# Two interleaved layers of long convolutions on one core: the order of issue taken from two stored tables

## The chip, the cores and the metric

The kernel runs on one core of one Trainium2 chip. The metric is the device time of one execution in microseconds, the median over the runs shown. A core has a matrix engine (PE, TensorE), a vector engine (DVE, VectorE), a scalar engine (ACT, ScalarE), a general engine (POOL, GpSimd) and a queue engine (SP, SyncE) which here issues nearly all transfers. Each engine works through its own instructions strictly in the order in which they were issued to it; they meet at semaphores.

## The reference

The input x has 2048 positions and 512 channels. Four layers are added to it in turn, A, B, A, B, each fed with the layer norm of x:

```python
def _A_ref(q, k, v, shift_k, ssm_k, ssm_D):        # gate by q, filter given
    k_shift = causal convolution of k with 4 taps per channel
    kv = k_shift * v
    y = causal convolution of kv with ssm_k, 2048 taps per channel (FFT)
    return q * (y + kv * ssm_D)
def _B_ref(u, log_A_real, A_imag, C_real, C_imag, log_dt, D_skip):
    dt = exp(log_dt); A = -exp(log_A_real) + 1j * A_imag; C = (C_real + 1j * C_imag) * dt
    K[d, l] = 2 * Re sum_n C[d, n] * exp(A[d, n] * dt[d] * l)          # 128 modes, 2048 taps
    return causal convolution of u with K (FFT) + u * D_skip
x = A_q
x = x + _A_ref(_layernorm(x), A_k, A_v, A_shift_k, A_ssm_k, A_ssm_D)
x = x + _B_ref(_layernorm(x), B_...)
x = x + _A_ref(_layernorm(x), A_k, A_v, A_shift_k, A_ssm_k, A_ssm_D)
x = x + _B_ref(_layernorm(x), B_...)
```

The convolution inside A does not depend on x, so both A layers share it: it is done once, and each A layer then only scales x by rows and channels. B's filter K is the same in both B layers as well.

## The kernel before

All data is float32. A convolution over 4096 points is a two-stage transform on TensorE, with 32 by 32 transposes on VectorE between the stages. Channels go in four quarters of 128, a quarter in four groups of 32.

The names of tiles, which the profile shows, are the way to follow the work:

- *The filter of B* (`taps`: `load_rows`, `mags`, `angles`, `waves`, `products`, `contract`): 64 steps. SP loads mode rows (`rw`) from a DRAM array (`rows_d`) that the setup has written; TensorE makes magnitudes (`pm`) and angles (`pa`); ScalarE takes exponentials (`m`) and sines (`ab`, `tt`); POOL and VectorE multiply (`xy`, `e`); TensorE sums over modes (`pk`); VectorE scales (`ks`) and SP stores the taps (`kdram`).
- *The two filters' spectra* (`spectrum_quarter`): load (`kk`), transform (`pf`, transposes to `zk`, `pu`), copy (`pc`), store in DRAM (`spec`). Quarter by quarter, A's from the input, B's from `kdram`.
- *kv of A* (`gated`): load (`kvt`), four products on POOL (`prod`) that TensorE adds up (`kv`), store (`kv_d`).
- *A convolution* (`convolution`, once for A, twice for B), 32 steps of four frequencies: `pf`, `zu`, `pu` forward; multiplication by the loaded spectrum (`kab`; `vv`, `sw`); inverse by `pi`, a copy (`zu` or `ie`), transposes (`w`), `po`. For A, `finish_a` keeps the result (`ya`, stored in `ya_d`) and updates the loaded quarter of x (`xq`, from which POOL has subtracted the row mean); a quarter of x is stored as `x1_d`.
- *Between the layers*: row statistics (`st`, `mv`), the normalizer (`var`, `rs`, `nb`) and normalized rows (`u`). The second A layer is `gated_update`.

None of this is issued in the order in which it is written. Engines are stand-ins: `record` (line 151) notes each operation with what it reads and writes. `flush` (line 475) asks `best` for an order, and then issues all operations in it, chaining those of each engine so that the order holds. There are two flushes. The first covers everything up to the normalized and transformed first quarter of the first B layer (2211 operations, of which the first 63 are setup that was issued directly); the second covers both B layers and the second A update (824 operations).

`plan` (line 279) is a list scheduler: at each step it takes, over all engines, the operation that can start first by the cost model, and among those of one engine with the same start the one with the lowest rank. `best` (line 442) first plans with the rank of recording, then 24 times with ranks made from the latest starts (`latest`) and the starts of the last plan, and keeps the plan with the shortest modelled length. `plan` also picks the buffer of the shared PSUM tiles (tags `c1`, one bank, and `f1`, two double banks in the first flush). The cost model is in `cost` (line 192): per operation the time that it occupies its engine, its latency, and for transfers the time on a common server.

## Time and profile before

| | us |
|---|---|
| median of 3 runs (671.56 to 673.98) | 671.78 |
| the profiled execution, its own time | 677.28 |
| its span from first to last instruction | 675.5 |
| first operations of the second flush in the trace | 456 |

The page of the profile gives busy time by engine, the span in 40 slices, the groups of instructions by operation and tile, and the transfers. As one helper records every operation, nearly all have one line (L487), so groups are told apart by tile names. Tiles that share a buffer can show under one name: `pm` and some `pu` of the first half stand as `pf`, and `po` as `kv`. A float32 matmul shows as two instructions. The stretches that the prediction uses are: up to 60 us the setup and the first spectra; to 236 us the filter of B, the spectra and kv together; to 408 us A's convolution beside the rest of B's filter; to 460 us the passage to the first B layer; to 510 and 578 us the first B convolution and the second A update; to 663 us the second B convolution; then the last outputs.

### The profile page before, as it was taken

To read this page: it belongs to the slowest core of one execution; us is meant where nothing else is said; L and a number is where in the kernel's file an instruction comes from. 1 tells how busy PE (TensorE), PEld (TensorE's weight loads), DVE (VectorE), ACT (ScalarE), POOL (GpSimd) and SP (SyncE) were. 2 spreads that over 40 slices of the span, in tenths; PEclk is the share of its full clock that TensorE was granted. 3 is DMA by queue.
4 is the path that set the end of the run, shared out by engine and by line. 5 is a ranking of instruction groups with operands and counts; after the bars stand their busy time and mean duration, and the time that the engine had idled before them with its cause. 6 is when DMAs were issued, how large, how long until landed. Compare 5 with 4: busy or idle time off the path is not lost. (4 is left out here: it accounts for less than half of the span.)

```text
span 675.5 us, 20764 instructions
## 1 busy us (share of the span) xinstructions
PE 532.5 (79%) x8568; PEld 300.0 (44%) x8568; DVE 472.1 (70%) x900; ACT 409.1 (61%) x770; POOL 352.9 (52%) x344
## 2 busy tenths in 40 slices
PE   1468979988999998888797884546989932799994
PEld 0123444534444366454555641414656601467571
DVE  7514746664467686798797896544569999898884
ACT  3304877886767799886557772355744408937341
POOL 3445887898879774551633554003536410366461
PEclk9969989998999999897998886657999965989998
DMA  7887997797877376469677743795677421077875
GB/s 214 219 227 217 258 225 247 220 257 172 231 230 242 119 252 215 140 169 270 207 258 188 235 143 91 224 318 207 257 277 250 163 94 62 2 244 250 294 236 109
DMA packets 74499, 138.97 MB, mean 206 GB/s; under 512 B 8092, under 2 KB 37156, under 8 KB 72356
## 3 DMA queue, kind: packets, MB, share of 16 engines
q1 hardware_dynamic: 73540, 135.21, 66.0%
q0 software_dynamic: 864, 2.43, 1.3%
q8 instruction: 68, 1.11, 0.7%
q14 instruction: 27, 0.22, 0.1%
HBM read 97.75 MB, written 39.85 MB: 204 GB/s over the span
## 5 line engine op out<-in xcount | busy, mean ns | idle before, releaser
L487 POOL TENSOR_TENSOR xy<-tt,m 128x512 f32<-128x512 f32 x128 | 148.6, 1184 | 87.8 <-issue 37.9
L487 POOL TENSOR_TENSOR sw<-sw,kab 128x512 f32<-128x512 f32 x64 | 81.3, 1291 | 104.4 <-ACT sw L487 93.6
L487 POOL TENSOR_TENSOR prod<-kvt 128x512 f32<-128x512 f32 x64 | 80.1, 1272 | 12.3 <-PE pf L487 4.2
L487 DVE STREAM_TRANSPOSE zu<-pf 128x512 f32<-128x512 f32 x96 | 62.7, 691 | 19.4 <-PE pf L487 16.3
L487 PE MATMUL kv<-prod,minus 128*128 128x512 f32 x128 | 72.3, 660 | 2.9 <-DVE prod L487 2.9
L487 PE MATMUL pf<-u,w 64*128 64x512 f32 (+1 forms) x200 | 60.5, 692 | 16.0 <-ACT u L487 11.2
L487 PE MATMUL pf<-kk,w 64*128 64x512 f32 x128 | 43.7, 720 | 31.8 <-DMA kk<-ssmk_in 19.3
L487 ACT COPY pc<-pf 128x512 f32<-128x512 f32 x64 | 35.8, 591 | 52.5 <-PE pf L487 34.1
L487 ACT COPY ie<-pi 128x1024 f32<-128x1024 f32 x32 | 32.4, 1013 | 53.1 <-PE pi L487 53.1
L487 DVE STREAM_TRANSPOSE zk<-pf 128x512 f32<-128x512 f32 x64 | 42.0, 694 | 32.1 <-PE pf L487 30.5
L487 ACT ACTIVATE m<-pf 128x1024 f32<-128x1024 f32 x48 | 47.7, 1027 | 23.4 <-PE pf L487 22.9
L487 DVE TENSOR_TENSOR vv<-pu,kab 128x512 f32<-128x512 f32 x64 | 41.8, 678 | 27.9 <-ACT sw L487 22.9
L487 DVE TENSOR_TENSOR e<-pa,m 128x512 f32<-128x512 f32 x64 | 43.4, 680 | 21.4 <-ACT pa L487 14.4
L487 ACT ACTIVATE ab<-pa 128x512 f32<-128x512 f32 x64 | 38.3, 598 | 28.4 <-PE pa L487 28.2
L487 PE MATMUL pi<-vv,mm 64*64 64x128 f32 x1024 | 52.9, 275 | 1.6 <-DVE vv L487 0.8
L487 DVE TENSOR_SCALAR y<-pa 128x512 fp32r<-128x512 f32 x64 | 43.1, 681 | 12.0 <-PE pa L487 11.2
L487 PE MATMUL pi<-sw,mm 64*64 64x128 f32 x1024 | 51.5, 269 | 0.0
L487 PE MATMUL pk<-xy,e 128*32 128x64 f32 x2048 | 45.3, 235 | 4.3 <-POOL xy L487 3.0
L487 PEld LDWEIGHTS pk<-xy,e 128*32 128x32 f32 x2048 | 34.8, 118 | 28.6 <-issue 16.9
L487 PE MATMUL pu<-zu,w 64*64 64x128 f32 x1024 | 35.5, 275 | 12.3 <-DVE zu L487 7.4
L487 ACT ACTIVATE u<-x,nb,rs 128x128 f32<-128x128 f32 x101 | 40.5, 483 | 7.5 <-DMA x<-x_d 6.3
L487 ACT COPY sw<-pu 128x1024 f32<-128x1024 f32 x32 | 32.1, 1013 | 21.0 <-PE pu L487 18.9
(121 smaller groups left out, 1088.1 us busy)
## 6 DMA issues: line engine op xcount, KB each, us to landing
kab<-spec SPq DMA_DIRECT2D x94, 512.0 KB, 4.8
spec<-pc SPq DMA_DIRECT2D x64, 256.0 KB, 4.4
kvt<-kv_in SPq DMA_DIRECT2D x32, 312.0 KB, 6.2
kk<-ssmk_in SPq DMA_DIRECT2D x32, 128.0 KB, 8.7
xr<-x_in SPq DMA_DIRECT2D x8, 512.0 KB, 6.3
kv_d<-prod SPq DMA_DIRECT2D x16, 256.0 KB, 3.1
kdram<-ks SPq DMA_DIRECT2D x64, 64.0 KB, 4.4
kk<-kdram SPq DMA_DIRECT2D x32, 128.0 KB, 2.8
```

The lines of the kernel that those rows point to most:

```text
L487: ins = getattr(self.engines[op.engine], name)(*a, **k).ins
```

## The change

Two lists are put into the kernel. A list names the recorded operations of one flush by their numbers (the place at which `record` met them), in an order over all engines. `best` no longer searches: it hands `plan` the rank of each operation in the list. `plan` still takes the earliest possible start first, so the list decides among operations of one engine that could start at the same time. `latest` and `TURNS` go. In the cost model, the rate of a transfer now depends on its direction and on the length of its contiguous pieces, a transfer takes 0.6 us longer, and one case of ScalarE's cost is counted otherwise. In `prepare`, a recorded operation now comes, for the plan, after the operations of its engine that were issued before it; `flush` makes no edge of that, as it does so between different engines alone.

```diff
+ORDERS = [
+    [
...
+        131, 72, 76, 73, 108, 89, 107, 85, 121, 74, 86, 115, 75, 232, 116, 153, 144, 88, 134, 112, 87, 135, 278,
+        145, 138, 132, 154, 139, 146, 130, 91, 155, 77, 133, 140, 95, 147, 123, 92, 141, 78, 136, 277, 97, 358,
+        137, 142, 122, 143, 93, 109, 231, 357, 117, 111, 94, 110, 276, 150, 118, 148, 149, 162, 158, 96, 322,
...
+        1860, 1853, 1859, 1852, 2004, 2073, 1884, 2042, 2002, 1885, 1858, 1855, 2043, 1886, 1856, 1857, 1894,
+        1889, 1861, 1895, 1888, 1887, 2005, 2076, 1891, 1893, 1900, 1892, 2003, 1890, 2077, 1911, 1910, 1901,
+        1955, 1909, 2078, 1896, 2079, 2008, 1956, 2045, 2009, 1912, 2044, 2046, 2006, 1957, 2047, 1902, 1960,
+        2048, 2007, 1905, 1903, 1904, 1906, 2049, 1907, 1965, 1908, 1959, 2051, 1966, 1958, 1964, 1962, 1974,
...
+    ],
+    [
...
+        147, 119, 152, 151, 141, 157, 156, 153, 158, 154, 166, 148, 142, 149, 177, 159, 162, 155, 173, 175, 167,
...
+        739, 741, 748, 747, 719, 752, 750, 740, 751, 759, 753, 758, 755, 746, 757, 762, 760, 754, 761, 733, 763,
+        768, 769, 756, 766, 767, 734, 764, 776, 765, 735, 770, 736, 772, 777, 786, 742, 773, 785, 779, 775, 798,
...
+    ],
+]
...
             size = 4 * int(np.prod([c for _, c in aps[0].ap]))
             run = min(self.run(x) for x in aps)
-            return (450 if op.engine == "D" else 600), 1500 + size / 290, size / (290 if run >= 512 else 200)
+            if aps[0].space != DRAM:
+                rate = 340 if run == 1024 else 228 if run == 1248 else 268 if run > 2000 else 279
+            else:
+                rate = 211 if run < 512 else 322 if run < 1024 else 350
+            return (450 if op.engine == "D" else 600), 1500 + size / rate, size / rate
...
-            if any(hasattr(k.get(x), "tensor") for x in ("scale", "bias")):
-                o = n / 1.2 + (186 if name == "activation" and len(big) == 1 else 280)
+            given = sum(hasattr(k.get(x), "tensor") for x in ("scale", "bias"))
+            if given:
+                o = n / 1.2 + (186 if given == 1 else 280)
...
         self.costs = [self.cost(op) for op in ops]
+        issued = {}
+        for op in ops:
+            if op.engine in issued:
+                op.ordered.append(issued[op.engine])
+            if op.ins is not None:
+                issued[op.engine] = op
...
             if op.calls[0][0] == "dma_start":
                 server = max(server, t + o) + extra
-                end[n] = max(t + o + 1500, server + 1200)
+                end[n] = max(t + o + 2100, server + 1800)
...
-    def latest(self):
...
-    TURNS = 24
-
     def best(self):
-        order = self.plan()
-        best = self.length, order, self.place, self.starts, self.ends
-        for turn in range(self.TURNS):
...
-        self.length, order, self.place, self.starts, self.ends = best
-        return order
+        return self.plan(list(np.argsort(ORDERS.pop(0))))
```

What the numbers named later are, in the first list: 128 to 131 row loads of B's filter (`rw`), 132 to 143 its first magnitudes (`pm`, `m`), 144 and 153 its first angles (`pa`), 162 the first product (`xy`), 73 and 86 the first `pf` groups of A's filter spectrum, 2002 to 2005 the four transfers of the last quarter of x (`xq`), 2006 to 2009 the subtractions on it, 2047 a store of `ya`, 2183 to 2204 the `pf` of the first B quarter, 2190 the second of them. In the second list: 162 to 175 statistics (`st`) of the first B layer, 735 and 736 stores of outputs, 756 and 761 the last loads of the spectrum (`kab`). A place on an engine, as the prediction uses it, is the rank of an operation among the recorded operations of its engine, counted from 0, in the list or in the trace of before.

More of the change, by code (lines that the diff above doesn't have):

```diff
@@ L440 @@
-    TURNS = 24
-    def best(self):
-        order = self.plan()
-        best = self.length, order, self.place, self.starts, self.ends
-        for turn in range(self.TURNS):
-            late, early = self.latest(), self.starts
-            if turn % 3 == 2:
-                place = sorted(range(len(late)), key=lambda n: late[n])
-                rank = [0.0] * len(late)
-                for i, n in enumerate(place):
-                    rank[n] = i + n
-            else:
-                rank = [l + (e if turn % 3 else l) for l, e in zip(late, early)]
-            order = self.plan(rank)
-            if order is None:
-                break
-            if self.length < best[0]:
-                best = self.length, order, self.place, self.starts, self.ends
-        self.length, order, self.place, self.starts, self.ends = best
-        return order
+    def best(self):
+        return self.plan(list(np.argsort(ORDERS.pop(0))))
```

28 lines of the change are left out of this document (removed), and 148 rows, old and new, of the table ORDERS.

## The prediction

> **What bounds the kernel now.** I read the page's busy shares first, then the table by stretches of time, and then the timeline of single engines in the stretches that are not full.
>
> ```profile
> span 675.5 us, 20764 instructions
> PE 532.5 (79%) x8568; PEld 300.0 (44%) x8568; DVE 472.1 (70%) x900; ACT 409.1 (61%) x770; POOL 352.9 (52%) x344
> ...
> 0.00:34.00 34.00, 9.55 (x15) 3.13 (x16) 20.73 (x33) 11.35 (x17) 13.27 (x27) 1.00 0.79 217
> 34.00:60.00 26.00, 17.07 (x97) 7.13 (x96) 7.87 (x16) 3.55 (x6) 12.91 (x15) 0.80 0.73 208
> 60.00:236.00 176.00, 165.00 (x1968) 77.83 (x1966) 102.82 (x175) 133.87 (x271) 144.99 (x137) 0.96 0.79 223
> 236.00:408.00 172.00, 147.82 (x2960) 93.42 (x2960) 143.51 (x259) 130.89 (x261) 83.56 (x79) 0.91 0.69 207
> 408.00:460.00 52.00, 26.26 (x264) 13.32 (x264) 24.90 (x72) 20.77 (x47) 7.28 (x10) 0.65 0.69 213
> 460.00:510.00 50.00, 41.52 (x914) 28.75 (x916) 32.03 (x48) 27.67 (x44) 25.17 (x20) 0.93 0.64 234
> 510.00:578.00 68.00, 41.94 (x686) 23.86 (x682) 64.32 (x184) 31.98 (x53) 20.24 (x20) 0.80 0.40 140
> 578.00:663.00 85.00, 78.13 (x1658) 51.28 (x1658) 71.50 (x113) 47.88 (x74) 42.88 (x38) 0.98 0.65 210
> ```
>
> Columns of a stretch: its length, then busy time of PE, PEld, DVE, ACT and POOL, the granted TensorE clock, the DMA share, GB/s. No engine bounds the whole. TensorE is full from 60 to 236 us (165.0 of 176, 94%) and nearly so from 578 to 663 (92%). VectorE is full from 510 to 578 (64.3 of 68, 95%). Between 236 and 408 TensorE (86%) and VectorE (83%) share the load and neither is full: 24 and 28 us of waits on one another. Before 60 and from 408 to 460 every engine is under 70%: latencies in a row. An order can gain only where nothing is full, or by moving work out of a full stretch into a free one. It removes no instruction, so the busy sums stay.
>
> **The change, part by part.** All sums are against the profiled execution: 675.5 us of span, 677.28 us of its own time, 5.5 above the median of 671.78.
>
> *Planner edits.* The transfer rates, the two added fixed 0.6 us, ScalarE's cost and the removed `latest` are arithmetic at build time; no edge comes from the new `issued` chain either, since `flush` writes `op.ordered` edges only between different engines. Cost 0. They act only through the order and through which PSUM buffer a shared tile gets.
>
> *Start of the first table.* Recorded numbers tell what is moved. On SP the row loads 129, 128 and 131 of the generator stand at places 7, 8 and 10 of the planned transfers; in the trace they were at 32, 37 and 31. On TensorE the first `pa` and `pm` matmuls (153, 144, 134) stand at places 2 to 4, against 18 to 20, ahead of all but two `pf` groups of the filter spectrum. On POOL the first `xy` product (162) is at place 14, against 33.
>
> ```profile
> 21.90 4.70 SPq L179 DMA_DIRECT2D rows_d<-hl  x3
> 47.13 3.43 SPq L487 DMA_DIRECT2D rw<-rows_d  x4
> DMA to landing us min/median/max: 2.1/3.1/4.1
> kk<-ssmk_in SPq DMA_DIRECT2D x32, 128.0 KB, 8.7
> 14.78 2.07 PE L487 MATMUL pf<-kk,w 64*128 64x512 f32 x2 [14.78 <-DMA kk<-ssmk_in]
> 26.52 5.62 PE L487 MATMUL pf<-kk,w 64*128 64x512 f32 x10 [9.68 <-POOL kk L487]
> 39.96 2.17 PE L487 MATMUL pf<-kk,w 64*128 64x512 f32 x4 [4.53 <-DMA kk<-ssmk_in]
> 50.03 1.13 PE L487 MATMUL pf<-kk,w 64*128 64x512 f32 x4
> 58.10 0.73 PE L487 MATMUL pf<-tg,rw 64*128 64x512 f32 x4
> 72.31 4.62 POOL L487 TENSOR_TENSOR xy<-tt,m 128x512 f32<-128x512 f32 x4
> ```
>
> The rows are in DRAM soon after 26.6 us (21.90 + 4.70), plus a store's landing, which no row gives; I take 4 us, an estimate from the 2.1 to 4.1 us of their loads. The loads then land between 34 (3.1) and 39 us (8.7, the median of the crowded `kk` queue). The first generator matmul starts then, not at 58.1; the way from it to the first `xy`, 72.31 - 58.10 = 14.2 us, stays: first `xy` at 47 to 54 us, some 20 us earlier. That is not 20 us of span. TensorE had done 9.55 + 17.07 = 26.6 us by 60 and then ran at 94%. In the new order it waits for the rows with two groups done, so `pf` and `kv` work that filled 26 to 58 us stands behind: it loses 34 - 28 = 6 to 39 - 28 = 11 us of filling, and gains what the earlier generator gives it, at most the 26.0 - 17.07 = 8.9 us it idled from 34 to 60. At 236 us the same work precedes the first convolution step in both orders. So this part lies between -9 and +11 us; I take 0, in the middle, because 94% leaves little. Cover: what stands behind the row loads on SP is `kvt` and `kk`, whose users move behind too.
>
> The stretch from 34 to 60 us has a granted clock of 0.80, and the two rows of four `pf` matmuls are 2.17 us at 40 and 1.13 at 50. The Trainium skill ("TensorE: Matmul & The Clock Gate", What's actually happening) says that the clock falls to half after an idle window of about 3.4 us and rises after a busy one; the two rows agree. By that rule a thinner start stays cold for longer, which is the second rival below.
>
> *Middle, 236 to 408 us.* The table moves the convolution ahead of the last filters' spectra: its `zu`, `pi` and `w` steps of quarter 1 move 15 to 35 places forward on TensorE, VectorE and ScalarE, `pk` and `pu<-zk` back by as many; at quarter 3 only 3 to 10 places are left. What can be gained is the idle of the fuller engine, 172 - 147.8 = 24 us, of which the forward moves can reach about the half that is not handed back by the end: bounds 0 and -12. I take -4, nearer to 0, since the displacement shrinks to a third at the end of the stretch.
>
> *End of the first table.* This is a chain that the trace shows whole:
>
> ```profile
> 393.30 0.34 SPq L487 DMA_DIRECT2D x_d<-xq  x1
> 397.90 1.25 SPq L487 DMA_DIRECT2D xq<-x_in  x2
> 402.44 0.36 SPq L487 DMA_DIRECT2D ya_d<-ya  x1
> 402.86 0.53 SPq L487 DMA_DIRECT2D xq<-x_in  x1
> 404.61 0.54 SPq L487 DMA_DIRECT2D xq<-x_in  x1
> 407.27 1.19 POOL L487 TENSOR_TENSOR xy<-tt,m 128x512 f32<-128x512 f32 x1 [0.49 <-POOL xy L487]
> 408.40 4.05 POOL L487 TENSOR_TENSOR xq<-xq,off 128x512 f32<-128x512 f32 x4
> 412.48 0.69 DVE L487 SCALAR_TENSOR_TENSOR xq<-kv,xq 128x512 f32<-128x512 f32 x1 [3.43 <-POOL xq L487]
> 435.66 2.77 SPq L487 DMA_DIRECT2D x<-x_d  x2
> 424.70 2.15 PE L487 MATMUL pf<-kk,w 64*128 64x512 f32 x4 [0.97 <-DMA kk<-kdram]
> 445.38 2.08 PE L487 MATMUL pf<-u,w 64*128 64x512 f32 x4 [10.52 <-ACT u L487]
> ```
>
> The last quarter of x is loaded in four pieces. After two, SP stood at the store of `ya` (402.44), whose copy was late, and the fourth piece left at 404.61. The table has all four in a row (2004, 2002, 2005, 2003), ahead of that store (2047): the fourth goes at about 397.9 + 4 x 0.6 = 400.3. That is 4.3 us earlier, and the four subtractions, VectorE's update, the store of x1 and its reload hang on it. Bounds 0 (POOL or the bank is late instead) and -4.3; I take -4.3, as VectorE waited 3.43 for exactly this. What is late next is the `w`, `po`, `ya` round. Behind the reload the table puts the normalizer and the `u` rows ahead of the spectrum's last `pc` copies, but one `pf` (2190) behind them: 0 us, bounds -3 (the `pf` idle of 10.52 is mostly the reload, which stays) and +5 (the last `pf` waits for four pairs of `pu`).
>
> *Second table.* Everywhere under ten places, except in two spots.
>
> ```profile
> 493.00:510.00 17.00, 0.00 (x0) 1.00 0.59 214
> 510.00:527.00 17.00, 2.92 (x13) 1.00 0.90 309
> 646.19 1.75 SPq L487 DMA_DIRECT2D out_dram<-yo  x2
> 648.71 7.32 DMA kab<-spec
> 656.05 0.69 DVE L487 TENSOR_TENSOR vv<-pu,kab 128x512 f32<-128x512 f32 x1 [0.39 <-DMA kab<-spec]
> ```
>
> The first two rows are the `st` statistics alone (VectorE's busy time in a stretch): none before 510 us, 2.92 us in the full stretch that follows. The table puts nine of them (162, 173, 175, 172 and others) up to 30 places forward, among work that ran at 507 to 514. VectorE has 50 - 32.0 = 18 us free from 460 to 510, so what is moved there shortens the full stretch: bounds 0 and -2.9, I take -2. Late next is the rest of VectorE's own row of work to 578. At the end, the last `kab` load (761) was issued at 648.71 behind two output stores, landed after 7.32 us, and VectorE waited for it. The table has it in front of those two: up to 648.71 - 646.19 = 2.5 us, if its buffer is free by then; I take -1.5, between -2.5 and 0.
>
> **Sum.** 0 - 4 - 4.3 + 0 - 2 - 1.5 = -11.8 us: 665.5 for an execution like the profiled one, 660.0 for the median. The ends add to -9 - 12 - 4.3 - 3 - 2.9 - 2.5 = -33.7 and +11 + 5 = +16; they will not all fall on one side. The forecast's own range is 646 to 668 us.
>
> **Rivals.**
> *The generator is the clock of the first stretch.* If the convolution's start at 236 us waits for POOL's products rather than for TensorE, the 20 us by which `xy` starts earlier come through. For it: POOL is 145.0 of 176 us busy there and starts late. Against: 82% is less than TensorE's 94%, and POOL's last `kv` products keep nearly their places. Half of the 20 us more: about 650 us. Chance 0.15.
> *A cold, thin start.* TensorE waits for the rows to 39 us and the eight groups behind run at the clock of the row at 39.96. It then brings 11 us less to 60 us, all paid at 94%: 671.8 - 11.8 + 11 = 671 us. For it: the `kk` queue's 8.7 us. Against: the row loads' own 3.1. Chance 0.11. This is also what no change would look like.
> *The last filter spectrum ends the first half (slower).* On POOL the table puts the four subtractions (2008, 2009, 2006, 2007) ahead of ten `xy` products, nine of which ran before them. If the x pieces land no earlier than now, POOL stands until 408.4 with those ten behind: 412.4 + 10 x 1.19 = 424 instead of 413.5, and the chain `pk`, `ks`, store, load, `pf` (now 424.70) slips by some 10 us, past the `u` work, with `pf` 2190 behind it. It decides from the point where the convolution is less than about 8 us ahead at 393 us. The gain of 4.3 is lost, the middle's 4 with it (it is its condition), and 10 is added: 671.8 - 3.5 + 10 = 678 us. For it: POOL runs in order and has ten products there. Against: the middle moves the convolution forward. Chance 0.16.
>
> **Chances.** Forecast 0.58, larger gain 0.15, cold start 0.11, slower 0.16. The range of 8 in 10 runs from 645 (the larger gain, nearly whole) to 677 us. Within 0.5% (668.4 to 675.1), about what a measurement of this kernel tells from no change, lies the cold start; above it the slow rival and a little of the cold start; the rest is faster.
>
> **What will show it.** In the changed profile: the first `rw` load at 30 us and the first `xy` at 47 to 54; TensorE's busy time by 60 us near 26 (the start is 0), under 20 (cold) or over 30; the first `pi` matmul before 236 us or not; four `xq` loads without a store between them, and `xq` subtractions within 8 us of the first load; `st` busy before 510; the last `kab` load issued before 647. The prediction is wrong if the busy shares from 60 to 236 fall, or if POOL waits for `xq` with `xy` behind it.

## The result: 0.77% faster, where 1.75% was forecast

| | before | changed |
|---|---|---|
| median, us (20 runs each) | 675.19 | 669.14 |
| lowest to highest | 670.01 to 687.34 | 664.66 to 677.50 |
| ratio changed to before, 95% interval | | 0.9923 (0.9894 to 0.9951) |
| span of the profiled execution, us | 675.5 | 666.4 |

The changed kernel is faster by 5.2 us (0.0077 x 675.19; 3.3 to 7.2 us by the interval). The medians, here and below, are over all runs, while the ratios leave out slow runs, those more than 1.5% above the fastest of the same kernel, so a ratio is not the quotient of two medians. The forecast was 11.8 us. In the 20 runs the kernel before has a median of 675.19 and not the 671.78 of the three runs that the forecast started from, so the time of 669.14 lies in the range given, and yet the step to it is 44% of the forecast. The two profiled executions differ by 9.1 us, more than the medians do.

The page's first lines of the changed kernel, and then the table by stretches as for the kernel before (length; busy time of PE, PEld, DVE, ACT, POOL; granted TensorE clock; DMA share; GB/s):

```profile
span 666.4 us, 20761 instructions
PE 525.2 (79%) x8568; PEld 292.3 (44%) x8568; DVE 474.5 (71%) x900; ACT 409.3 (61%) x770; POOL 352.5 (53%) x344
```

```profile
0.00:34.00 34.00, 5.85 (x8) 1.67 (x8) 19.03 (x31) 11.36 (x17) 10.83 (x25) 1.00 0.59 164
34.00:60.00 26.00, 20.50 (x118) 8.15 (x122) 7.53 (x12) 14.26 (x25) 13.63 (x13) 1.00 0.92 201
60.00:236.00 176.00, 167.39 (x2221) 81.22 (x2213) 112.02 (x196) 131.71 (x268) 152.26 (x145) 1.00 0.88 250
236.00:408.00 172.00, 142.57 (x2680) 85.14 (x2676) 140.13 (x249) 120.83 (x241) 78.11 (x74) 0.89 0.66 193
408.00:460.00 52.00, 26.37 (x329) 13.23 (x329) 26.70 (x77) 27.66 (x62) 11.39 (x12) 0.74 0.71 222
460.00:510.00 50.00, 45.44 (x1008) 30.41 (x1012) 39.03 (x64) 25.11 (x35) 25.29 (x21) 1.00 0.78 271
510.00:578.00 68.00, 43.73 (x641) 24.86 (x636) 61.27 (x179) 38.24 (x74) 17.43 (x21) 0.82 0.29 102
```

The work is the same. What differs early is the granted clock: 1.00 from 34 to 236 us, where the kernel before has 0.80 and 0.96. What differs late is little: the stretch from 408 to 460 is as empty as before (26.37 us of TensorE against 26.26).

Rows picked from the timelines of the changed kernel's engines, at the places that the prediction named (start, length, engine, operation; in brackets the idle time before it and what ended it):

```profile
13.75 12.71 SPq L345 DMA_DIRECT2D rows_d<-hl  x4
34.16 0.81 SPq L615 DMA_DIRECT2D rw<-rows_d  x2
42.19 4.95 POOL L615 TENSOR_TENSOR prod<-kvt 128x512 f32<-128x512 f32 x4 [15.45 <-DMA kvt<-kv_in]
50.46 2.31 POOL L615 TENSOR_TENSOR xy<-tt,m 128x512 f32<-128x512 f32 x2 [3.13 <-ACT tt L615]
227.20 0.45 PE L615 MATMUL pf<-vv,mm 64*64 64x128 f32 x8 [0.43 <-DVE zk L615]
384.50 2.60 SPq L615 DMA_DIRECT2D xq<-x_in  x4
393.66 4.03 POOL L615 TENSOR_TENSOR xq<-xq,off 128x512 f32<-128x512 f32 x4
417.76 1.78 SPq L615 DMA_DIRECT2D kdram<-ks  x4
421.73 0.56 SPq L615 DMA_DIRECT2D x<-x_d  x1
422.53 2.78 SPq L615 DMA_DIRECT2D kk<-kdram  x2
429.81 0.34 POOL L615 TENSOR_TENSOR kk<-kk,dr 1x32 f32<-1x32 f32 x1 [16.13 <-DMA kk<-kdram]
443.98 0.58 ACT L615 COPY pc<-pf 128x512 f32<-128x512 f32 x1 [2.09 <-DMA spec<-pc]
445.83 2.08 PE L615 MATMUL pf<-u,w 64*128 64x512 f32 x4 [3.94 <-ACT pc L615]
449.49 1.99 PE L615 MATMUL pu<-zu,w 64*64 64x128 f32 x32 [1.58 <-DVE zu L615]
```

The rows of the kernel before that answer to these and that the prediction did not show:

```profile
236.33 0.45 PE L487 MATMUL pf<-vv,mm 64*64 64x128 f32 x8 [0.74 <-DVE vv L487]
418.17 1.76 SPq L487 DMA_DIRECT2D kdram<-ks  x4
421.46 1.16 SPq L487 DMA_DIRECT2D kk<-kdram  x2
424.06 0.24 POOL L487 TENSOR_TENSOR kk<-kk,dr 1x32 f32<-1x32 f32 x1 [10.30 <-DMA kk<-kdram]
455.95 1.11 PE L487 MATMUL pu<-zu,w 64*64 64x128 f32 x32 [1.51 <-DVE zu L487]
```

Read as a lead over the kernel before, the rows tell the case. The generator's first `xy` leads by 21.9 us (72.31 - 50.46), the first `pi` (shown as `pf<-vv,mm`) by 9.1, the reload of x by 13.9 (435.66 - 421.73), and the first product of the second half by 6.5 (455.95 - 449.49). So half of what convolution A had won was gone 28 us later. The last filter's chain never had that lead: its last taps are stored at 417.76 instead of 418.17. It then fell 5.8 us behind: its `kk` loads stand on SP behind the first reload of x (422.53), and POOL has them at 429.81 instead of 424.06. Everything after hangs on it: the pairs `pu<-zk`, their evictions `pc`, which wait for the store of `spec` (443.98), and the last `pf<-u` (2190), which the table puts behind those pairs and which waits 3.94 us for a PSUM buffer.

### The profile page after: what moved, and what is told of

Same layout as the page of the kernel before. It is cut to its first block, busy times and chain, and to the rows that moved or that the text cites. A ratio compares the mean times of both kernels' runs of the same rounds, so it can differ in the third digit from the quotient of the medians.

```text
span 666.4 us, 20761 instructions
## 1 busy us (share of the span) xinstructions
PE 525.2 (79%) x8568; PEld 292.3 (44%) x8568; DVE 474.5 (71%) x900; ACT 409.3 (61%) x770; POOL 352.5 (53%) x344
## 4 chain that ended last, share of the span: by engine, by line
PE 35%; DVE 17%; ACT 9%; DMA 8%; issue 4%; POOL 2%; SPq 1%; DVEq 0%; ACTq 0%; POOLq 0%
PE pf L615 11%; PE pi L615 6%; PE kv L615 6%; DMA kab<-spec 5%; PE po L615 4%; PE pu L615 3%; PE pa L615 3%; DVE zu L615 3%; DVE st L615 3%; PE pk L615 3%; DVE x L615 2%; DVE vv L615 2%; ACT tt L615 2%; ACT m L615 1%; DVE sw L615 1%
## 5 line engine op out<-in xcount | busy, mean ns | idle before, releaser
L615 PE MATMUL pf<-kk,w 64*128 64x512 f32 x128 | 45.8, 729 | 42.3 <-DMA kk<-kdram 14.8
L615 PE MATMUL pf<-u,w 64*128 64x512 f32 (+1 forms) x200 | 56.7, 651 | 13.3 <-ACT pc L615 3.9
L615 ACT ACTIVATE tt<-pa 128x256 f32<-128x256 f32 x128 | 46.6, 387 | 22.4 <-PE pa L615 22.1
L615 ACT COPY sw<-pu 128x1024 f32<-128x1024 f32 x32 | 32.3, 1016 | 27.2 <-PE pu L615 23.1
L615 PE MATMUL pa<-tt,rw 64*128 64x512 f32 x64 | 34.1, 537 | 17.1 <-DVE e L615 8.8
```

Of the source, the lines that this page charges most:

```text
L615: ins = getattr(self.engines[op.engine], name)(*a, **k).ins
```

## The experiments

The kernels below are the changed kernel with edited lists. In the shortened code below, names such as FIRST_TABLE stand for whole lists, and of the lists by engine only the part that differs stands there. A switch makes each engine take its operations exactly as they stand in the list:

```diff
+        line = {e: sorted((op.n for op in ops if op.engine == e), key=lambda n: -rank[n]) for e in self.engines}
...
                 for n in l:
+                    if self.STRICT and n != line[e][-1]:
+                        continue
```

With it, and a second switch for the old cost model, the order of the kernel before is a list too; with both tables as they stand the switch gives the changed kernel's own order and buffers.

| run | median, us | ratio to the kernel before (95%) |
|---|---|---|
| changed kernel, first | 669.14 | 0.9923 (0.9894 to 0.9951) |
| changed kernel, again | 666.88 | 0.9886 (0.9826 to 0.9945) |
| first table only | 666.99 | 0.9877 (0.9830 to 0.9925) |
| second table only | 677.09 | 0.9972 (0.9933 to 1.0011) |
| head of the table, rest as before | 690.04 | 1.0140 (1.0059 to 1.0222) |
| filter tail mended (m2) | 667.24 | 0.9855 (0.9804 to 0.9906) |
| filter tail, second (m4) | 667.60 | 0.9897 (0.9840 to 0.9954) |
| products at 27 us (m5) | 673.11 | 0.9935 (0.9898 to 0.9972) |
| m4 and m5 (m6) | 674.07 | 1.0004 (0.9965 to 1.0042) |
| changed, kept warm (w1) | 671.40 | 0.9923 (0.9881 to 0.9965) |
| m5, kept warm (w2) | 670.95 | 0.9922 (0.9869 to 0.9974) |
| before, kept warm (w3) | 677.84 | 1.0021 (0.9966 to 1.0077) |
| old order from 588 us (s1) | 665.53 | 0.9839 (0.9775 to 0.9903) |
| m4 and old order from 588 us (c1) | 665.44 | 0.9842 (0.9792 to 0.9892) |

A single execution of one more kernel (x1) took 669.87 us.

### One table alone

```diff
-ORDERS = [FIRST_TABLE, SECOND_TABLE]
+ORDERS = [FIRST_TABLE, ORDER_OF_BEFORE_2]     # first table only
+ORDERS = [ORDER_OF_BEFORE_1, SECOND_TABLE]    # second table only
```

> The first half issued by the table, the second half (the second list) in the order of the kernel before. Theory A, the gain is made in the first half and part of it is handed back at its end: the trace after stands 13 to 16 us ahead at the x updates and only 6.5 us ahead at the first product of the second half, so this kernel should be faster than the one before by most of the whole change's gain: ratio 0.993 to 0.996. Theory B, the first table gives what the profiled execution says (9 us or more) and the second table loses it: ratio 0.988 or lower. Theory C, the first table gives nothing and the second all: ratio 1.000.

> The first half in the order of the kernel before, the second half issued by the table. Theory A: the second table gives the 2.6 us by which the profiled execution grew its lead after the first product of the second half, near the 3.5 us forecast for it: ratio 0.995 to 0.998. Theory B, it loses: ratio 1.003 to 1.008. Theory C, it is the whole gain: ratio 0.992.

> The changed kernel as it is, as the mark for the runs beside it: ratio to the kernel before 0.990 to 0.994. Were it 0.985 to 0.988, the whole change would be worth as much as the first table alone was in its run (0.988), and the difference between the two would be the scatter of the kernel before.

The first table alone is as fast as both (0.9877 beside 0.9886 and 0.9923). That is theory B's number for it (0.988 or lower), and A's 0.993 lies outside its interval. The second table alone is worth 1.9 us (0.0028 x 677.79), between a gain of 4.5 and a loss of 0.7: theory A's number, against B's loss. So neither of the two holds whole, and theory C falls. The first table was forecast at 8.3 us and measured 8.3 (0.0123 x 677.79, between 5.1 and 11.5) in this run; that is luck, as its terms were off one by one (below). The changed kernel again gave 7.7 us (0.9886, just outside the 0.990 to 0.994 expected), and 5.2 in its first 20 runs: the forecast is missed by less, or by more, with the run of the kernel before that stands beside it.

The run with the second table only also shows how far two executions of one order differ. Its first half is the old order, and yet the timeline of its TensorE has the first `pi` and the first product of the second half here:

```profile
230.38 0.45 PE L614 MATMUL pf<-vv,mm 64*64 64x128 f32 x8 [0.74 <-DVE vv L614]
...
447.44 1.70 PE L614 MATMUL pu<-zu,w 64*64 64x128 f32 x32 [1.78 <-DVE zu L614]
```

That is 6.0 and 8.5 us ahead of the kernel before with not one instruction moved. A lead read from two executions carries that much chance, so the table below averages: the two executions with the old first half (before, second table only) against six with the first table unedited (changed, again, first table only, w1, x1, s1), from the same row of each.

| first instruction of | old order, us | first table, us | lead |
|---|---|---|---|
| `pi`, first | 233.4 (230.4 to 236.3) | 227.3 (226.8 to 228.0) | 6.1 |
| store of the third x1 quarter | 390.1 | 378.2 | 11.9 |
| store of the last filter's taps (`kdram`) | 414.6 (411.0 to 418.2) | 416.9 (412.6 to 420.5) | -2.3 |
| reload of x | 431.7 (427.8 to 435.7) | 420.9 (416.6 to 424.5) | 10.8 |
| first product of the second half | 451.7 (447.4 to 456.0) | 448.7 (444.3 to 452.5) | 3.0 |

One distance hardly varies at all: from the reload of x to the first product of the second half it is 19.6 and 20.3 us with the old order, and 27.5 to 28.1 us in all six with the table; two more kernels with the table's tail (m5 and w2, below) have 27.7 and 27.6, and two more with the old tail (head of the table and w3) 20.2. The table's tail costs 7.8 us of lead each time. The third row says why there was something to lose: the table brings the reload of x 10.8 us forward and the last filter's taps 2.3 us back, and the second half needs both.

### The tail of the first half

The first mended tail (m2), by engine, as the lists now stand:

```diff
 SP:   2063,
-      2139, 2104, 2105, 2140, ...
+      2104, 2105, 2139, 2140, ...
 PE:   2107,
-      2183, 2197, 2124, 2204, 2119, 2134, 2129, 2190
+      2124, 2119, 2183, 2197, 2204, 2190, 2134, 2129
 DVE:  2109, 2108 (zk) ahead of 2168 (first u)
 ACT:  2127, 2125, 2122, 2120 (pc) ahead of 2167 (first u)
```

> Both tables, with only the end of the first one changed: the two loads of the last filter's lags (kk) ahead of the reload of x on SP, their transposes ahead of the normalised x on VectorE, two of the four pairs pu<-zk ahead of the first pf<-u on TensorE with their evictions ahead of the normalised x on ScalarE, and the last pf<-u of the quarter ahead of the other two pairs. Theory A, the last filter's spectrum holds the second half (the third rival of the prediction, on top of the gain of the start): the first product of the second half comes 5 to 8 us earlier than the 449.5 us of the trace after, and the kernel is that much faster than after: ratio to the kernel before 0.981 to 0.986. If the wait moves to the PSUM buffers of the last two pairs, 2 to 3 us: 0.988. Theory B and C, the end of the first half isn't where the gain went: ratio as after, 0.992.

Three rows of m2's timelines, of POOL, SP and TensorE:

```profile
424.10 0.24 POOL L614 TENSOR_TENSOR kk<-kk,dr 1x32 f32<-1x32 f32 x1 [10.03 <-DMA kk<-kdram]
435.88 11.24 SPq L614 DMA_DIRECT2D spec<-pc  x8
446.79 1.11 PE L614 MATMUL pu<-zu,w 64*64 64x128 f32 x32 [1.24 <-ACT pc L614]
```

The `kk` of the last filter are there at 424.10, 5.7 us sooner than in the changed kernel although x was reloaded 0.9 us later. But the copies of the first pairs, done by 433.4, cannot be stored until 435.88, since SP is still at the reloads of x; the second four wait for their buffers, and the first product of the second half waits for `pc`. It comes 24.1 us after the reload of x instead of 27.8: 3.7 us of the 7.8 are back. In absolute time it is 2.7 us sooner than in the changed kernel, the number of the expectation's second case and not of theory A; the ratio, 0.9855, is in theory A's range, but its interval (0.9804 to 0.9906) reaches the second case's 0.988.

The second mended tail (m4) takes that queue as well:

```diff
 SP:   ... 2104, 2105, 2139, 2140,
-      2141, 2142, 2128, 2126, 2123, 2121, ...
+      2128, 2126, 2123, 2121, 2141, 2142, ...
 PE:   2107, 2124, 2183, 2197, 2119, 2204, 2190, 2134, 2129
 ACT:  three u, 2127, 2125, five u, 2122, 2120
```

> As the first mended tail, with the queue that held it mended as well: there the first four stores of the last spectrum stood on SP behind three reloads of x, from 431 until 436 to 441 us, and the four pairs' evictions behind them on their buffers. Here these stores come ahead of the third and fourth reload of x, and ScalarE makes half of the first normalised u before it evicts. Theory A (the last filter's spectrum holds the second half): first product of the second half at 441 to 445 us where the trace after has 449.5, and a time 4 to 8 us under that of the changed kernel beside it. If that lead is handed back again by the end, as with the first mended tail (2.7 us ahead at the first product, 1 us behind at the last store), the second half has an end of its own that the first doesn't move: time within 2 us of the changed kernel's.

The timelines of SP and TensorE in m4:

```profile
427.55 9.09 SPq L614 DMA_DIRECT2D spec<-pc  x4
444.43 1.87 PE L614 MATMUL pu<-zu,w 64*64 64x128 f32 x32 [4.35 <-ACT pc L614]
```

The first product is at 444.43, inside the 441 to 445 expected; but the changed kernel's second run, with no edit, has it at 444.29, so that says little. It is 25.3 us behind the reload: no better than m2, and it waits 4.35 us for the same eviction. So one part of the give-back is shown by experiment (move the filter's loads, and 2 to 4 us of it return). The rest was not removed by any run: the taps come late, and four pairs, four copies' worth of buffers and a store's way through DRAM stand behind them.

Neither mended tail shows in the time: 667.24 and 667.60 beside 666.88 and 669.14. That is the second alternative of m4's expectation: a lead at the first product does not show at the end. So it is not shown either that the 7.8 us lost at this border are what the time lost.

### The start

```diff
-ORDERS = [FIRST_TABLE, SECOND_TABLE]
+ORDERS = [FIRST_TABLE[:198] + rest of ORDER_OF_BEFORE_1, ORDER_OF_BEFORE_2]
```

> The first 60 us of the first table (198 operations, to the first products of the positions' generator), and behind it every remaining operation of both halves in the order of the kernel before. My forecast put the start at 0; the rival took the generator as the clock of the first stretch and gave it 10 us or more. If the start is what the first table is worth, this kernel is 6 to 10 us faster than before (ratio 0.985 to 0.991), more than the whole table, since the end of the first half is then the old one; if the start is worth nothing, ratio 1.000; if the head start melts away on the way because other engines set the pace of conv A, 0.996 to 1.000, with the lead shrinking from 15 us at the first products to under 3 us at the x updates.

It is 9.5 us slower than before (0.0140 x 677.79), which no alternative had. Its stretch from 60 to 100 us and its TensorE timeline say why:

```profile
60.00:100.00 40.00, 29.31 (x301) 14.06 (x301) 18.95 (x38) 15.01 (x35) 22.70 (x23) 0.82 0.91 257
```

```profile
72.46 3.38 PE L614 MATMUL kv<-prod,minus 128*128 128x512 f32 x4 [6.55 <-POOL prod L614]
```

The old order behind the new head lets TensorE stand 6.55 us for `prod`, and it then runs at half rate: four `kv` in 3.38 us, which at 76.80 take 1.98. The clock of the stretch is 0.82, and 22 us of head start at the first `xy` become 9 us of delay by 89 us. A head start is worth nothing by itself; it must keep TensorE fed.

Next, POOL as the clock of the first stretch, by moving its products:

```diff
 SP:   84,
-      129, 128, 90, 131, 76, 89, 107, ..., 77, 123, 78
+      90, 89, 107, 78, 77, 129, 128, 131, 76, ...
 POOL: 91, 95, 97, 93,
-      117, 162, 163, 79, 196, ..., 102, 104, ..., 81
+      79, 102, 104, 81, 117, 162, 163, 196, ...
 PE:   92, 94 behind 134; 96, 98 behind 132; 80, 82, 103, 105 behind 140
```

> Both tables, with the start changed: four loads of kvt and one of kk, which stood behind the first rw on SP (34 us, it waits there for the stores of rows_d), are issued ahead of it at 26.5 us, and GpSimd's first eight products stand together ahead of its first xy. If GpSimd is the clock of the first stretch (the first rival of the prediction), its first product starts near 33 us where the trace after has 42.2, the last product on it and conv A's start come 4 to 8 us earlier, and the kernel is 3 to 7 us faster than the changed kernel beside it, less what the end of the first half hands back. If the positions' generator is the clock (its first products stay at 36 to 50 us), nothing moves behind 100 us: same time within 1.5 us.

> The second mended tail and the changed start together. If start and tail are two ends of one chain that the last filter's spectrum closes, the two gains add: 7 to 14 us under the changed kernel. If the second half has its own end or the lead melts in conv A, no better than the better of the two alone.

The timelines of POOL and TensorE in m5:

```profile
27.36 9.81 POOL L614 TENSOR_TENSOR prod<-kvt 128x512 f32<-128x512 f32 x8
76.23 2.08 PE L614 MATMUL pf<-kk,w 64*128 64x512 f32 x4
229.86 0.45 PE L614 MATMUL pf<-vv,mm 64*64 64x128 f32 x8 [0.43 <-DVE zk L614]
```

POOL's products start at 27.36 instead of 42.19, and the first `pi` comes later (229.86 against 227.20), not sooner: these products are not what it waits for. (The first `xy`, behind them now, comes at 53.77, 3.3 us later than in the changed kernel.) At 76 us TensorE is at half rate (2.08 us for four `pf`), where the changed kernel takes 1.13. The third kernel (m6), with both edits, gains from neither: at 674.07 it is slower than the changed kernel beside it and level with the kernel before (1.0004). That was not expected, and it is only described: its first `pi` comes at 232.37, and its second half takes 221.7 us from the first product to the start of the last store, where the two runs of the changed kernel take 213.5 and 217.3.

Whether the rate is the price can be tested by feeding TensorE in its pauses with products of constants that the next operation overwrites:

```diff
+            for _ in range(FILL.pop(n, 0)):
+                to = self.move(op.calls[0][1][0])
+                to = bass.AP(to.tensor, 0, [[to.ap[0][0], 128], [1, 512]])
+                ins = self.engines["T"].matmul(to, w, tg, start=True, stop=True).ins
...
+FILL = {153: 6}                           # w1: changed kernel
+FILL = {153: 6, 109: 1, 166: 2, 265: 2}   # w2: m5
+FILL = {118: 6, 166: 2}                   # w3: the kernel before
```

> Both tables, and six products of constants (128x512, into the PSUM buffer that the next operation overwrites) put on TensorE ahead of its first generator product, where it stands idle from 30 to 36.6 us; nothing else is changed, and the results aren't touched. In the trace after, TensorE's products run at half rate until 51.4 us (a pair kv<-prod takes 2.07 us there and 0.98 us later). Theory: the first stretch is paced by TensorE and by the rate that it is granted; then the half-rate products from 36 to 51 us go, the first xy comes 3 to 5 us earlier than 50.5 us, and the kernel is 2 to 5 us faster than the changed one (ratio to the kernel before 0.982 to 0.987). If the generator is paced by ScalarE and GpSimd (between its products TensorE waits for m and prod), the rate changes and the times behind 60 us don't: ratio as the changed kernel, 0.989 to 0.992.

> The changed start of m5 (kvt loads and eight products early), with the same six products of constants ahead of the first generator product and five more at the pauses at 50, 53 and 72.6 us. m5 ran 40 to 100 us with the products at 76, 85 and 88 us at half rate and lost 2.7 us of its lead there. If that is why it was 6 us slower than the changed kernel beside it, no product from 55 to 100 us is at half rate and the ratio to the kernel before is 0.983 to 0.988; and if GpSimd's early products are worth anything at all, lower than w1. If m5's order itself is worse, its ratio stays: 0.992 to 0.995.

> The kernel before in its own order, with six such products in TensorE's pause from 35.4 to 40 us and two in that at 42 to 43.5 us. In the trace of before, its products run at half rate from 40 to 49 us, and a third of the first hundred us is below full rate. If the rate is what the new start is worth, most of the first table's gain can be had with the old order: ratio 0.990 to 0.995, with the products of 75 to 100 us 3 to 5 us earlier. If the order is what it is worth (the generator starting at 36 and not at 60 us), ratio 0.998 to 1.002: the next wait (the products' loads, until 53 us) takes the place of the half rate.

w1 did not do what it was made for. Its six products ran at once and were over by 32.3 us, as TensorE's timeline in w1 shows:

```profile
29.38 2.93 PE L619 MATMUL pa<-tg 128*128 128x512 f32 x6
36.23 0.76 PE L624 MATMUL pa<-tt,rw 64*128 64x512 f32 x1 [3.93 <-DMA rw<-rows_d]
43.24 2.08 PE L624 MATMUL kv<-prod,minus 128*128 128x512 f32 x2 [1.15 <-POOL prod L624]
```

A pause of 3.93 us remained, the pair of `kv` took 2.08 us as without them, and the time says nothing on the theory. w2 did; POOL and TensorE in its timeline:

```profile
26.81 9.84 POOL L624 TENSOR_TENSOR prod<-kvt 128x512 f32<-128x512 f32 x8
75.08 1.13 PE L624 MATMUL pf<-kk,w 64*128 64x512 f32 x4
227.00 0.45 PE L624 MATMUL pf<-vv,mm 64*64 64x128 f32 x8 [0.43 <-DVE zk L624]
```

With the pauses fed, the `pf` at 75 us is at full rate and the first `pi` is back at 227.00, 2.9 us ahead of m5 and level with the changed kernel. How much of that is rate can be added up from the traces, if each operation's shortest duration in the sixteen is taken as its full rate: up to the first `pi`, m5 runs slower than that by 13.3 us in all, w2 by 9.3; m5 stands for 16.3 us, w2 for 17.4 (the constants' products counted as standing). The changed kernel has 14.3 and 12.6. So the constants win back rate, but what m5 lost against the changed kernel is standing, and POOL's 15 us of earlier products were worth nothing on top of it. In the time w2 is 670.95 against 673.11, with intervals that overlap, and its ratio, 0.9922, is that of the alternative by which m5's order itself is worse. w3 is no faster than before, as its second alternative said; but its constants removed only 1.4 us of slower running (15.2 us against 16.6), so what full rate would be worth in the old order stays open.

### The end of the second half

With the second table the second half seems to gain at first and then to give it back. From its first product to the `pi` of group 546 the nine executions with the whole second table take 132.7 to 136.1 us, before 138.0 and first table only 137.4; from there to the start of the last store they take 80.1 to 86.2 us, against 78.2 and 77.5. But the kernel with the head of the table, whose second half is the old order too, takes 135.1 and 82.9. So the split is not the second table's alone.

One part of the later stretch is a stand of TensorE with no cause that the profile shows. The waits of TensorE on nothing shown, from 590 to 662 us, in the changed kernel, in its second run, with the first table only and with the head of the table (us in total, times, longest):

```profile
PE pi L615 <- issue: 1.6, 1, 1.6
```

```profile
PE pi L614 <- issue: 2.7, 1, 2.7
```

```profile
PE pi L614 <- issue: 0.2, 1, 0.2
```

```profile
PE pu L614 <- issue: 2.6, 1, 2.6
```

All nine executions with the whole second table and no shift have such a stand of 1.2 to 2.7 us in the middle of the same operation near 636 us, some a second one; first table only has 0.2 us in another operation, and before none. The last row is of the kernel with the head of the table, so of the old order, and its stand is in another operation: the second table is not the cause of such stands. Two tests, one that shifts TensorE's stream by 64 small products, one that puts the old order back for the last 262 operations:

```diff
+            if not ORDERS and n == 420:                # x1
+                for _ in range(32):
+                    ins = self.engines["T"].matmul(idle[:, :64], w1, w1[:, :64], start=True, stop=True).ins
...
-ORDERS = [FIRST_TABLE, SECOND_TABLE]
+ORDERS = [FIRST_TABLE, SECOND_TABLE[:562] + rest of ORDER_OF_BEFORE_2]      # s1
+ORDERS = [FIRST_TABLE of m4, SECOND_TABLE[:562] + rest of ORDER_OF_BEFORE_2]   # c1
```

> Both tables, and 32 products of a constant by 64 of its columns (64 recorded products, and as many weight loads) on TensorE ahead of its first idle product of the second half, where it stands idle from 541 to 555 us. In every profiled execution with the second table TensorE stands 1.2 to 2.7 us in the middle of one pi<-mm,vv near 636 us, waiting for nothing that the profile shows, behind the 8190th of the kernel's products; the shorter stands lie multiples of 128 or 129 products away from it. If the stand belongs to a place in TensorE's stream of instructions, it moves to 64 of the kernel's products earlier (behind the 8126th, some 3 us sooner). If it belongs to what that product needs, it stays behind the 8190th.

> The first table, the second one up to 588 us, and from there on the remaining 262 operations in the order of the kernel before. With the second table the lead over the kernel before grows by 2 to 5 us up to the pi<-mm,vv of 594 us (normaliser and its statistics), and shrinks by 1 to 7 us from there to the last store; with the old order it stays as it is. If the last 80 us of the second table are what it loses, this kernel keeps the gain: 1 to 4 us under the changed kernel, ratio 0.982 to 0.988. If the loss is the end's own (a last chain that is as long in either order), as the changed kernel: 0.989 to 0.992.

> The same with the second mended tail of the first half. If the mended tail's lead (2.5 to 3.5 us at the first product of the second half) was lost only in the second table's last 80 us, it is kept here: ratio 0.978 to 0.985. If it is lost at the start of the second half (spectra stored late, so kab late), as s1.

TensorE's waits in x1, from 600 us on:

```profile
PE pu L622 <- DVE vv L622: 2.3, 1, 2.3
PE po L622 <- DVE w L622: 1.8, 2, 1.2
```

The stand is gone from its operation, with order, operands and waits as they were: it doesn't belong to the operands. It did not reappear 64 products earlier either, in this one execution. The runs with added constants answer the question instead: w1 has six more products in front and w2 eleven, and the stand comes 6 and 10 products sooner within the same operation (behind its 40th and 36th product, elsewhere behind its 46th). It belongs to a place in TensorE's stream; the last section counts it. s1 and c1 have the lowest medians of all, 665.53 and 665.44, with ratios of 0.984. Their intervals reach into that of the changed kernel's second run, so that they beat it is likely, not proved. By the expectations these ratios are those of a gain that is kept; the traces do not bear out the reason: from group 546 to the last store their executions take 81.7 and 83.0 us, 3.5 to 5.5 more than before and first table only, as the others do, with a stand in another operation (1.2 and 1.7 us). The old order of the end is thus not shown to be the cure that the expectation had in it. (The traced execution of s1, 672.28 us, is the longest of its six.) The mended tail adds nothing to s1.

## Why the prediction was right in sign and wrong in size

By its own terms, with the averaged leads above; terms in us, gain negative:

| step | forecast (bounds) | measured |
|---|---|---|
| start of the first table | 0 (-9 to +11) | -6.1 |
| middle | -4 (-12 to 0) | -5.8 |
| `xq` chain | -4.3 (-4.3 to 0) | +1.1 |
| behind the reload | 0 (-3 to +5) | +7.8 |
| second table | -3.5 (-5.4 to 0) | -1.9 |
| sum | -11.8 | -4.9 |

The `measured` column is the differences of the leads (11.9 - 6.1, then 10.8 - 11.9, then 3.0 - 10.8) and the time of the second table alone. Its sum is close to the 5.2 us of the 20 runs, but that is less of a proof than it looks: the first four rows add to -3.0, while the first table alone measured -8.3 (-11.5 to -5.1) in time. The old order's side of the leads is two executions that are 8.5 us apart at the border, so the first row and the sum may be some 4 us off; the fourth row, a distance within each execution, is not touched by that. The old side is in fact early: the traced execution with the second table only is the fastest of its twelve (669.71 us; median 677.09). Against the kernel before alone the four rows are -9.0, -6.1, +0.4 and +7.5 and add to -7.2, near the -8.3. So most of the 5 us between -3.0 and -8.3 comes from the choice of executions, and the first row may be as large as 9 us.

*The step that failed is the one behind the reload.* It was priced at 0 with +5 as its worst, because the normalizer and `u` were taken as the end of the half and the spectrum as a side matter. It costs 7.8 us and is outside its bound. The prediction named the place ("with `pf` 2190 behind it") in the slower rival, but gave it another cause: POOL's subtractions ahead of the `xy`. They did run there (393.66) and POOL then stood 2.32 us for ScalarE's `tt`, not for `xq`; they were not the price. What the runs show in its place has two parts. The last filter is a chain of its own, and the table gave it no lead: its taps are stored 2.3 us later than in the old order, while the reload of x comes 10.8 us sooner. And SP's order delays it further: the reload of x, early now, stands ahead of the filter's `kk`, which reach POOL 7.3 us after their issue (422.53 to 429.81; before 2.6), and the last `pf` stands behind the pairs. The second part is shown by m2 and m4 (3.7 and 2.5 us back); the first is read from the traces, and no run moved the taps. The rival's condition (convolution A less than 8 us ahead at 393 us) was not met, and its loss came all the same. Neither of the two signs that were to show the prediction wrong appeared: TensorE's busy time from 60 to 236 us rose (167.39 for 165.00), and POOL did not wait for `xq`; no sign was set on the filter's taps.

*The `xq` chain was 5.4 us too hopeful* (+1.1 for -4.3). Four loads in a row came true, and the fourth is 18.1 us ahead of before where the first is 13.4. The subtractions began 9.2 us after the first load, not within 8. But the last update and the store of x1 gained nothing by it: from the third x1 store to the fourth the lead fell from 11.9 to 8.4 us, and at the reload it was 10.8. What was "late next", the round of `w`, `po` and `ya`, was late at once. That a wait of 3.43 us is seen does not make it the last one.

*The start was priced too low, by about 6 us.* The first `pi` is at 226.8 to 228.0 us in all six executions with the table and at 230.4 and 236.3 with the old order, so the gain is 2.4 us at least. First `xy` at 50.46, inside 47 to 54; TensorE's busy time by 60 us 26.35 (5.85 + 20.50), the 26 that was to mean "the start is 0". That sign was a bad one: it counts time, not products. The rows' landing took 7.7 us after the store (34.16 - 26.46), not 4, without harm. Counted as work, each operation at its shortest duration in the traces, the six have done 23.1 to 24.8 us of it by 60 us, the old order 22.6 and 24.5: no gain so far, as forecast. By 100 us it is 63.3 to 64.4 against 58.2 and 61.6. So the gain lies behind 60 us, where the forecast left nothing because TensorE is 94% busy up to 236; from 60 to 100 us it is 87% in the kernel before (34.89 of 40). Most of the gain is less standing: up to the first `pi`, TensorE stands 20.5 and 15.7 us in the old order and 12.3 to 14.2 in the six, some 5 us less, and runs below its full rate by 16.6 and 15.4 us against 12.3 to 14.7, some 2 us less. That is the term of the prediction, filling lost against waits gained, with the wrong balance. The granted clock alone, 1.00 in all six from 60 to 236 us and 0.96 and 0.98 in the two old ones, would give the rate more (0.02 to 0.04 of 165.0 us is 3.3 to 6.6); the durations decide. The prediction had the clock only on the losing side, as a cold start. m5 and w2 show the rate at work within this step, and that POOL's products, had 15 us sooner, bring it nothing. The first rival foresaw a gain here, by a cause that no run bears out.

By the Trainium skill ("TensorE: Matmul & The Clock Gate", What's actually happening) the activity window runs freely and does not start with the work. This case agrees as far as it can: m5 and m6 share the same lists up to 400 us, and over 34 to 60 us their clocks are 1.00 and 0.93, and over 60 to 236 us 0.98 and 0.96.

*Middle:* -5.8 for -4, within its bounds. *Second table:* the `st` statistics moved as forecast, and the last `kab` loads were issued from 634.79 on in place of 648.71. VectorE waits for `kab` as long as before all the same: 2.5 us in three waits from 600 us on in both kernels, the last now at 638.41 and not at 656.05. First the changed kernel's `st` work alone in that stretch (VectorE's busy time), then SP's timeline:

```profile
493.00:510.00 17.00, 2.19 (x10) 1.00 0.70 225
```

```profile
634.79 5.49 SPq L615 DMA_DIRECT2D kab<-spec  x4
```

Both moves were made, and the second half from its first product to the start of the last store is 213.5 and 217.3 us in two runs of the changed kernel against 216.2 before. The stand near 636 us is 1.6 and 2.7 us of that. The rest is open.

## What to carry to other kernels

Where two chains meet at a border, price the border by the slower one: a lead counts only as far as both have it (here 10.8 us for one and -2.3 for the other), and moving one of them forward can also put its transfers ahead of the other's on the shared queue. A pause of TensorE costs its length and then the products that run at half rate after it (6.55 us, then 3.38 in place of 1.98, in the kernel with the head of the table), so an order is judged by whether it leaves pauses, and an early start that leaves one behind it can lose more than it brought. With executions of one order up to 8 us apart, compare distances within an execution (here reload to first product, steady to 0.6 us) before comparing absolute times.

## What was not expected of the hardware

*The granted clock can stand at 1.00 while products run at half rate.* The changed kernel shows 1.00 from 34 to 60 us, and in the same stretch TensorE's timeline has

```profile
43.51 2.07 PE L615 MATMUL kv<-prod,minus 128*128 128x512 f32 x2 [0.86 <-POOL prod L615]
52.65 1.98 PE L615 MATMUL kv<-prod,minus 128*128 128x512 f32 x4
```

the first row is two instructions, the second four, in the same time. The Trainium skill ("TensorE: Matmul & The Clock Gate", Seeing it yourself) warns that these events have been seen to be unreliable; here the durations decide.

*TensorE stands 0.4 to 2.7 us inside an operation, waiting for nothing shown, and always at the same places of its stream.* Counted are the entries that a trace has for TensorE, in the changed kernel 8568 products and, on the weight-load side, 8568 loads and 210 others, nearly all on semaphores. In the sixteen traces, the old order's included, every stand of over 0.4 us inside an operation from 100 us on comes behind an entry whose number is a multiple of 256 plus 193, to within one, whatever the operation there. Not every such place has a stand, and which has one changes from run to run. In the changed kernel they are the 6849th entry (299.9 us), the 11969th, the 12993rd and the 16577th (638.0 us): 20, 4 and 14 times 256 apart. In the page's list of DMA queues, the changed kernel's queue that loads instructions has (packets, MB, share)

```profile
q8 instruction: 67, 1.10, 0.7%
```

67 packets for 1.10 MB, 16.4 KB each; the 17346 entries are 67.8 times 256. The Trainium skill ("Runtime: NRT & Kernel Launch", Instruction fetch mechanics) says that an engine's instructions are fetched by transfers in blocks of 16 KiB, or 256 instructions, and that the cost at a boundary is mostly hidden. The stands are such blocks apart, and the packets are of that size and number; the stands say that here the cost is not always hidden, by up to 2.7 us. That they belong to places 256 entries apart is shown; that they are late fetches is an argument from these numbers, as no trace shows when an instruction arrives.
